# A two-layer spectral and mixer kernel: the d transform split in two steps, four w1 tiles in row halves, and new instruction orders

## The chip, the cores and the metric

The kernel runs on one core of one Trainium2 chip. The metric is the device time of one execution in microseconds. The kernel before the change was run three times: 343.45, 343.85 and 344.21 us, so its median is 343.85 us.

## What is computed

```python
def reference(A_x, A_w_r, A_w_i, B_x, B_w1, B_w2, B_w3, B_w4):
    def _A_ref(x, w_r, w_i):
        B, S, D = x.shape
        X = jnp.fft.rfft2(x.astype(jnp.float32), axes=(-2, -1))
        X = X * (w_r + 1j * w_i)
        return jnp.fft.irfft2(X, s=(S, D), axes=(-2, -1)).astype(jnp.bfloat16)
    def _B_ref(x, w1, w2, w3, w4):
        B, S, D = x.shape
        h = _gelu(_layernorm(x, axis=-1) @ w1)
        c = D // 4
        ...
        hs = jnp.concatenate([g0, g1, g2, g3], axis=-1) @ w2
        x1 = x + hs
        h2 = _gelu(_layernorm(x1, axis=-1) @ w3) @ w4
        return x1 + h2
    x = A_x
    x = x + _A_ref(_layernorm(x, axis=-1), A_w_r, A_w_i)
    x = x + _B_ref(_layernorm(x, axis=-1), B_w1, B_w2, B_w3, B_w4)
    x = x + _A_ref(_layernorm(x, axis=-1), A_w_r, A_w_i)
    x = x + _B_ref(_layernorm(x, axis=-1), B_w1, B_w2, B_w3, B_w4)
    return x
```

S is 2048, D is 512, the hidden width of w3 is 1792, and all inputs are bf16. The quarters g0 to g3 of h are shifted along the sequence by one row down, one up, two down and two up.

## The kernel before

The 2048 rows lie in SBUF as 16 groups "q" of 128 partitions each; row q of the text below means such a group. A layer is the spectral part (a two-dimensional Fourier transform, a product with W, the inverse transform) and the MLP part, and there are two layers; I call them layer 0 (ORDER_A) and layer 1 (ORDER_B).

**The order is written by hand.** Everything of a layer is one string of short operations, and a loop at the end of `layer` (L873) issues them one by one. A letter names the step, a number its tile, a last letter its engine (A for ACT, V for DVE, P for POOL, D for a form on DVE that reads PSUM), and a number after the dot the PSUM bank. Each engine runs its own operations in the order of the string; between engines, semaphores enforce the data dependences. ORDER_0 does the same for the first forward transform (`first_front`, L488). So the order decides what stands ahead of what in each engine's queue.

**The front.** For each row: statistics (`s` on DVE with bn_stats, or, for rows 1, 5 and 9, two sums on ACT), their aggregation (`i` on DVE), for the ACT rows the means and variances on POOL (`f`), the standard deviation per group of rows (`S` on ACT) and its reciprocal (`J` on DVE), then the transform table scaled by it (`Q`, on A, V or P), eight matmuls per row (`O`, L415 to L441), and the copy of the result from PSUM to the tile V (`G` and `L`; V has four parts t, and for split tiles `G` takes parts 0 and 1, `L` parts 2 and 3). One tile of the front is "plain": its right half is copied by ACT (`G3A`), the rest folded by DVE (`G3V`, L454, which writes V's parts 0 and 3 and a tile `pairs`), and a last fold `I` (L464) makes V's parts 1 and 2 out of `pairs`. The three ACT rows' `f2` also issues the first table DMAs on POOL. After ORDER_0 come `load_rest` and `load_mlp` (L553, L554).

**load_rest** (L194) stands in POOL's queue right after the front's last POOL step: a DMA that doubles the first quarter of W, `turn_TL` (L247, which makes the second half of TL for b under 8 out of the first), a second doubling, the DMA of TL2 (the second half of TL for b from 8), then two doublings and two loads of TR. `load_mlp` (L208) on SP waits for the last doubling and then loads G, Tinv and w1 to w3.

**The spectral part.** `d` (L582, four matmuls per b over V's four parts), `t` (its copy to TV), `q` (L602, matmuls of 64 rows that use TL's two halves), `x` (copy to X), `p` (the product with W, on V, P or D), `b` and `V` (L634, over TR), `m` and `l` (copies to hT), `D` and `C` (L656, over G), `Y` (copies), `P` (L679, over Tinv), `a` (L693, adds to x on DVE with a row sum). Units `u` of `d` and `q` hold one or two b's (UNITS, L892).

**The MLP part.** `s` squares on ACT, `r` statistics on POOL, `e` a square root on ACT, `i` the reciprocal, `M` and `n` normalize (A, V or P), `T` transposes two rows by DMA on SP into the tile xT, `v` (L727, w1: 8 matmuls of 512 columns over four rows, i.e. two transposes), `h` (gelu on ACT), `u` (L743, w2, reads neighbouring rows of h), `f`, `k`, `E`, `R`, `o`, `U` the same for the second normalization, `w` (L778, w3), `g` (gelu), `W` (L799, w4), `A` (adds to x). In layer 0 the next layer's front (`B`, `j`, `S`, `J`, `Q`, `O`, `G`, `L`, `I`) is interleaved with w3 and w4. ORDER_B begins with `X6`, six matmuls on zeros (`fill`, L272), and ends with the stores `y`.

Of the kernel before, what the change touches and what calls it, by code (L numbers as in the profile page):

```python
# [567 lines left out]
def layer(K, last):  # L568
# [13 lines left out]
    def over_d(u):  # L582
        bs = UNITS[u]
        ps["d", u] = o = banks(K, len(bs))
        for i, b in enumerate(bs):
            oi = o[:, i].rearrange("p (e r f) -> p e r f", e=2, r=4)
            part = lambda k: V[:, k, 2 * b:2 * b + 2].rearrange("d b q c -> d (b q c)")
            nc.tensor.matmul(oi[:, :, 3], lhsT=part(1), rhs=K.FL[:, 0:P].rearrange("p (e f) -> p e f", e=2),
                             start=True, stop=True)
# [82 lines left out]

    def fold_D(m):
        Y[m] = K.stream.tile([P, 2, 512], BF16, name="Y", tag="TV_Y", bufs=4, padded_shape=[P, 2, 512])
        o, r = ps.pop(("D", m))[:, :, 0:256], Y["r", m][:]
        for h, op in ((0, ALU.add), (1, ALU.subtract)):
            nc.vector.tensor_tensor(Y[m][:, :, h * 256:(h + 1) * 256], o, r, op=op)

    def back_p(q):  # L679
        ps["P", q] = o = banks(K, 1)[:, 0]  # L680
        y = Y[q // 2][:, q % 2]
        if q // 2 in FOLD[last]:
# [44 lines left out]
    def w1(k):  # L727
        g, h = divmod(k, 2)
        ps["v", k] = o = banks(K, 2)
        for i in range(2):  # L730
            j = 2 * h + i
            for t in range(4):
                nc.tensor.matmul(o[:, i], lhsT=K.w1[:, t, j * P:(j + 1) * P], rhs=xT[g][:, :, t, :],  # L733
                                 start=(t == 0), stop=(t == 3))
# [126 lines left out]
    def act_table(k):  # L861
# [5 lines left out]
    table = {"z": act_table, "e": lambda g: ln[g].std_twice(), "i": lambda g: ln[g].invert_twice(), "M": lambda g: ln[g].shift(), "J": invert4, "d": over_d, "t": take_d, "q": over_q, "x": take_q, "p": weigh, "b": lambda b: back_q(b, first_half(b)), "V": lambda b: back_q(b, 1),  # L867
# [4 lines left out]
             "O": front, "G": take_front, "L": lambda k, eng: take_front(k, eng, 1), "I": fold_front, "K": half_D, "H": fold_D, "N": negate}  # L872
# [31 lines left out]
FLEX = "mlGLnotxYIKEpQ"  # L904
FOLD = [(), ()]
ORDER_0 = """
s1 f0 s0 s3 s2 i3 i2 i0 s4 s5 S1 J1 s7 S0 J0 s6 i7 f2 Q2A Q3A i4 Q0A s9 i6 s8 O1.2 s11 f3 S2 J2 Q6P Q1A Q5A O0.4 i8
G1A Q4V O2.0 s10 i11 i10 S3 Q7P O3.2 G0A s13 J3 Q10V Q11A s12 s14 i12 O5.6 i14 G3A i13 G2A Q8P Q9P s15 S4 J4 O4.4 G5A
i15 Q12V Q13V S5 O6.0 L5A J5 Q14P O7.6 G4A G6A G3V Q15V L6V G7A O8.0 L7A G8A I3V L8A
"""  # L910
ORDER_A = """
d0.3 t0A d2.4 d1.2 d4.0 q0.6 t1V N0 t2A q1.2 d6.4 t4A q2.0 x1V x0V p1V t6A q4.2 d12.6 d10.4 x2A p2P p0V t12A t10A d8.0
p4D b0.6 d14.7 q10.4 m0V q6.2 t8A x10A t14A b1.0 b5.1 m5A m1A q12.4 q14.6 p6D b4.1 b2.0 p10V x14A p14P d15.2 m4A m2A
t15A q8.6 x8A b3.1 b7.0 m7A b11.2 q15.6 m11A x15A b10.3 b14.0 m3A b6.2 m6A p12D V12.4 b12.5 p8V p15V b13.7 b9.1 m10A
m12A b8.6 b15.2 m13V V15.3 m14V m9A m8V V13.5 V14.0 m15A D1.6 l12V D0.1 l15A l13A l14V C1 C0 Y0V Y1A D3.3 C3 P3.0 a3
P2.6 Y3A a2 s3 P0.5 a0 s2 P1.2 a1 s0 D2.0 C2 Y2V s1 r0 D5.6 C5 P7.2 a7 Y5A e0 s7 P6.4 D7.0 P4.5 a6 i0 M0 P5.2 D4.6 C4
P10.3 s6 C7 n2P a4 s4 a5 n3V n0V s5 Y4A D6.4 r1 P11.2 C6 P8.6 P9.7 e1 n1V a10 T1 Y7A P15.0 i1 M1 n5A s10 n4P n6P P14.1
Y6V P13.3 a8 s8 T0 a9 n7P s9 a11 P12.4 a15 s11 v1.6 r2 n10P T2 h1 T3 a13 a12 n11V c0 s15 T5 n8V v0.2 h0 s13 v3.4 n9V
v2.2 h3 u0.0 s12 h2 u1.4 a14 c1 s14 T4 u3.1 r3 f0 k0 n14V v5.2 n13A n15V T7 f1 E1V h5 f3 v4.6 u2.0 f2 E2V h4 c2 u6.6
f6 u5.5 f5 E5V k3 E6V n12P u7.0 E0V u4.1 f4 T6 v7.5 k2 k1 R0 E3V o2V o1V h7 o3A c3 v6.1 h6 o0P f7 u8.0 f8 E8P u13.5  # L920
u12.2 u11.6 u14.3 U1 f12 k4 k5 k7 f14 E14V k12 k6 u9.2 f11 u10.4 k8 E7V f13 k13 f10 R1 o7P o5P u15.3 E10V U0 w4.0 E4P
f9 E9P k11 f15 w2.4 g2 k10 o4V U2 w1.2 k14 g4 E15P k9 E13P w3.6 g3 g1 w5.0 w0.4 g0 w6.6 g5 g6 E11V W1.2 o6P U3 E12V A1
W3.6 A3 B3 B1 w8.0 W2.4 A2 W0.2 k15 R2 o10P o11A R3 o14V o9A g8 o12A w13.0 U5 w7.6 B2 g13 o8P U4 w15.4 w10.0 A0 B0 g10
w16.2 j1 g7 g16 w18.0 g18 w9.2 o15P w11.0 g9 w12.2 g12 j3 w17.6 j2 j0 S0 Q3V Q1V Q2P Q0V g11 W4.2 U7 O1.0 o13P g17 U6
A4 W7.3 B4 j4 G1A G1V A7 B7 j7 O0.0 w19.6 G0A W6.2 A6 g19 W5.3 A5 g15 B5 w23.4 g23 j5 B6 j6 S1 Q4P G0V w27.2 g27 I0V
w14.6 g14 Q5V O2.0 w20.2 w24.6 g20 W10.2 A10 B10 Q7V j10 W8.3 G2A A8 B8 W9.4 A9 B9 Q6V j9 W11.2 A11 w26.4 I1P B11 j11
g24 j8 O3.2 w22.6 S2 Q10P g26 G2V I2P Q11A Q8P g22 w21.0 g21 G3A w25.6 G3V g25 W12.0 A12 B12 j12 Q9P S12 J12 I3P O4.5
G4A Q12A G4V W15.1 A15 I4P B15 j15 W13.2 A13 S15 J15 B13 j13 W14.3 Q15P W24.2 S13 J13 Q13P O5.0 A14 A24 B14 B24 j14
G5A O15.4 G15V O6.2 S14 J14 L15A Q14A O14.4 G6A L6A G14A G5V I5V L14A
"""  # L930
# [47 lines left out]
```

## Time and profile before

| | |
|---|---|
| median of three runs | 343.85 us |
| the profiled execution's own time | 343.63 us |
| its span | 341.8 us |
| granted TensorE clock | 1.0 of full speed in every stage |
| TensorE idle before the first front matmul | 8.23 us from the start, 30 fill matmuls aside |
| first `d` matmul, layer 0 | 18.96 us |
| first `D` matmul, layer 0 | 36.87 us |
| first w1 matmul, layer 0 | 51.16 us |
| first `d` matmul, layer 1 | 182.08 us |
| last matmuls end | 339.1 us |

The busy time of an engine is the time in which one of its instructions ran; a matmul's row gives some 270 ns for 256 columns because it is pipelined, though the next one starts after 109 ns. So a busy TensorE is read by the distance from start to start. A waits view tells which engine sat idle for whom; a timeline shows one engine's instructions, start and duration in us, and in brackets the idle time ahead of it and what ended it.

### The profile page before, as it was taken

To read this page: it belongs to the slowest core of one execution; us is meant where nothing else is said; L and a number is where in the kernel's file an instruction comes from. 1 tells how busy PE (TensorE), PEld (TensorE's weight loads), DVE (VectorE), ACT (ScalarE), POOL (GpSimd) and SP (SyncE) were. 2 spreads that over 40 slices of the span, in tenths; PEclk is the share of its full clock that TensorE was granted. 3 is DMA by queue.
4 is the path that set the end of the run, shared out by engine and by line. 5 is a ranking of instruction groups with operands and counts; after the bars stand their busy time and mean duration, and the time that the engine had idled before them with its cause. 6 is when DMAs were issued, how large, how long until landed. Compare 5 with 4: busy or idle time off the path is not lost.

```text
span 341.8 us, 5734 instructions
## 1 busy us (share of the span) xinstructions
PE 334.3 (98%) x2184; PEld 186.8 (55%) x2184; DVE 163.5 (48%) x373; ACT 192.0 (56%) x356; POOL 117.5 (34%) x218
## 2 busy tenths in 40 slices
PE   6999999999999999999999999999999999999996
PEld 4878984444444444444467898444444444444443
DVE  4979895659034023535378979456901110200112
ACT  6989899665821542421628979986695132142310
POOL 3795067669633000402432505877722000000000
PEclk9999999999999999999999999999999999999999
DMA  7985936390231100000000003543130500000011
GB/s 261 313 284 197 339 78 117 71 270 19 46 61 31 32 0 0 2 0 0 2 0 2 2 3 64 104 83 61 33 61 0 125 31 0 15 17 32 15 63 46
DMA packets 45340, 24.60 MB, mean 72 GB/s; under 512 B 35153, under 2 KB 42321, under 8 KB 45313
## 3 DMA queue, kind: packets, MB, share of 16 engines
q1 hardware_dynamic: 43824, 19.74, 23.0%
q0 software_dynamic: 1248, 4.40, 3.9%
q8 instruction: 17, 0.28, 0.3%
q10 hardware_dynamic: 240, 0.10, 0.1%
q14 instruction: 11, 0.08, 0.1%
HBM read 11.61 MB, written 2.10 MB: 40 GB/s over the span
## 4 chain that ended last, share of the span: by engine, by line
PE 85%; ACT 8%; DVE 3%; DMA 2%; issue 1%; SPq 0%; ACTq 0%
PE ps L804 28%; PE ps L784 28%; PE ps L749 8%; PE ps L733 6%; PE ps L642 4%; ACT xn L303 3%; PE ps L612 2%; PE ps L594 2%; DVE x_state L698 2%; PE ps L662 2%; DMA x_state<-in_A_x_dram 1%; ACT hT L740 1%; DMA xT<-xn 1%; PE ps L439 1%; PE ps L429 1%
## 5 line engine op out<-in xcount | busy, mean ns | idle before, releaser
L791 ACT ACTIVATE gT<-ps 128x1024 bf16<-128x1024 f32 x56 | 55.7, 1023 | 97.6 <-PE ps L784 95.5
L804 PE MATMUL ps<-w,gT 128*128 128x512 bf16 (+2 forms) x476 | 99.4, 366 | 0.0
L784 PE MATMUL ps<-xT,w 128*128 128x512 bf16 x448 | 99.3, 379 | 0.0
L810 DVE TENSOR_TENSOR x_state<-ps,x_state 128x512 bf16<-128x512 f32 (+2 forms) x34 | 22.1, 659 | 123.4 <-PE ps L804 123.1
L804 PEld LDWEIGHTS <-gT 128*128 128x128 bf16 x476 | 45.4, 98 | 51.4
L784 PEld LDWEIGHTS <-w 128*128 128x128 bf16 x448 | 43.7, 98 | 52.1
L757 DVE SCALAR_TENSOR_TENSOR xn<-xn,ln_c,ps 128x512 bf16<-128x512 bf16 x32 | 23.3, 742 | 16.0 <-PE ps L749 6.3
L733 PE MATMUL ps<-xT,w 128*128 128x512 bf16 x128 | 28.6, 379 | 0.4 <-DMA xT<-xn 0.4
L749 PE MATMUL ps<-w,hT 128*128 128x512 bf16 x128 | 28.8, 379 | 0.1
L326 POOL TENSOR_SCALAR ln_ve<-ln_mv 128x4 f32<-128x4 f32 x11 | 3.0, 271 | 57.7 <-DVE ln_mv L319 57.0
L303 ACT ACTIVATE junk<-xn 128x512 bf16<-128x512 bf16 x32 | 19.8, 623 | 5.0 <-DVE xn L757 5.0
L291 DVE BATCH_NORM_STATS2 ln_st<-x_state 128x6 f32<-128x512 bf16 (+2 forms) x30 | 19.5, 665 | 3.5 <-DMA x_state<-in_A_x_dram 3.0
L698 DVE SCALAR_TENSOR_TENSOR x_state<-ps,x_state 128x512 bf16<-128x512 f32 x32 | 20.6, 684 | 0.9 <-PE ps L690 0.9
L733 PEld LDWEIGHTS <-w 128*128 128x128 bf16 x128 | 12.4, 98 | 15.6 <-DMA xT<-xn 1.0
L749 PEld LDWEIGHTS <-hT 128*128 128x128 bf16 x128 | 12.5, 98 | 15.4 <-ACT hT L740 1.0
L303 ACT ACTIVATE xn<-x_state 128x512 bf16<-128x512 bf16 x32 | 19.9, 626 | 0.8 <-DVE x_state L698 0.8
L740 ACT ACTIVATE hT<-ps 128x512 bf16<-128x512 f32 x32 | 17.6, 600 | 4.6 <-PE ps L733 4.5
L690 PE MATMUL ps<-Y,Tinv 128*128 128x256 bf16 x128 | 15.8, 272 | 0.4 <-DVE Y L152 0.4
L631 POOL TENSOR_TENSOR PB<-X,W 128x2048 bf16<-128x2048 bf16 (+1 forms) x4 | 12.1, 3033 | 11.2 <-DVE X L152 7.3
L154 ACT ACTIVATE TV<-ps 128x1024 bf16<-128x1024 f32 (+1 forms) x17 | 14.6, 895 | 2.4 <-PE ps L594 2.3
L642 PE MATMUL ps<-TR,PB 128*128 128x128 bf16 x256 | 15.9, 219 | 0.0
L662 PE MATMUL ps<-G,hT 128*128 128x256 bf16 x128 | 15.6, 273 | 0.0
(96 smaller groups left out, 414.0 us busy)
## 6 DMA issues: line engine op xcount, KB each, us to landing
w<-in_B_w_dram SPq DMA_DIRECT2D x4, 896.0 KB, 7.0
W<-W POOLq DMA_DIRECT2D x4, 514.0 KB, 5.1
x_state<-in_A_x_dram SPq DMA_DIRECT2D x8, 256.0 KB, 4.9
out_dram<-x_state SPq DMA_DIRECT2D x15, 128.0 KB, 1.8
w<-in_B_w_dram SPq DMA_DIRECT2D x4, 256.0 KB, 4.4
W<-in_A_w_r_dram SPq DMA_DIRECT2D x7, 128.5 KB, 5.4
W<-in_A_w_i_dram SPq DMA_DIRECT2D x7, 128.5 KB, 5.6
TL<-tab_TL POOLq DMA_DIRECT2D x3, 256.0 KB, 5.5
```

Source lines behind the costliest of these rows:

```text
L303: K.nc.scalar.activation(out, src, ACT.Square, bias=0.0, scale=D ** -0.5, accum_out=self.s[:, i, 1:2])
L642: nc.tensor.matmul(o[:, k0 * P:(k0 + 1) * P], lhsT=pab[u][:, k, 2 * (b - u) + h, f * P:(f + 1) * P], rhs=K.TR[:, k:k + 2, 2 * b + h], star ...
L662: nc.tensor.matmul(o[:, i, e * 256:(e + 1) * 256], lhsT=M[:, F, e, 2 * m + i, :], rhs=K.G[:, F, e, :], start=(F == 0 and e == 0), stop=(F ...
L698: nc.vector.scalar_tensor_tensor(K.x[:, q, :], ps.pop(("P", q)), 1.0, K.x[:, q, :], op0=ALU.mult, op1=ALU.add, accum_out=ln[g].s[:, i, 0:1])
L733: nc.tensor.matmul(o[:, i], lhsT=K.w1[:, t, j * P:(j + 1) * P], rhs=xT[g][:, :, t, :], start=(t == 0), stop=(t == 3))
L740: nc.scalar.activation(hv[:, 2 * h + i, 4 * g:4 * g + 4, PAD:PAD + P], o[:, i].rearrange("p (q c) -> p q c", q=4), ACT.Gelu_apprx_tanh, bi ...
L749: nc.tensor.matmul(o, lhsT=K.hT[:, j, st:st + P], rhs=K.w2[:, j, :], start=(j == 0), stop=(j == 3))
L757: nc.vector.scalar_tensor_tensor(xn[:, q, :], xn[:, q, :], ln[q // 4].c[:, q % 4:q % 4 + 1], ps.pop(("u", n)), op0=ALU.mult, op1=ALU.add, ...
L784: nc.tensor.matmul(o[:, i], lhsT=K.w3[:, c, t * P:(t + 1) * P], rhs=xT3[g][:, :, c, :], start=(c == 0), stop=(c == 3))
L791: nc.scalar.activation(gT[g][:, 2 * j:2 * j + 2, :], ps.pop(("w", k)), ACT.Gelu_apprx_tanh, bias=0.0, scale=1.0)
L804: nc.tensor.matmul(o, lhsT=gT[g][:, t, i * P:(i + 1) * P], rhs=K.w4[:, t, d], start=(t == 0), stop=(t == 13))
L810: nc.vector.tensor_tensor(x, ps.pop(("W", n)), x, op=ALU.add)
```

## The change

`over_d` becomes two operations: `d` multiplies V's parts 1 and 0, `F` parts 3 and 2 of the same bank. `w1` for k = 0 and 1 in each layer multiplies rows 0 and 1 (`v0`, `v1`) and rows 2 and 3 (`v8`, `v9`) separately. The tables get a way to fold the inverse transform on POOL (`whole_D`, `fold_P`, POOL_FOLD), which is empty and called by no order. All three orders are new; among others, the six fill matmuls of ORDER_B are gone, `I3` is on POOL in ORDER_0 and `Q14` there on ACT. Shown are the code and the parts of the orders that are spoken of.

```diff
--- before.py
+++ after.py
@@ -579,19 +579,23 @@
     ps = {}
     tv, X, pab, Y, xT, xT3, gT, ln, ln3, lnA = [{} for _ in range(10)]
 
-    def over_d(u):
+    def over_d(u, late):
         bs = UNITS[u]
-        ps["d", u] = o = banks(K, len(bs))
+        if not late:
+            ps["d", u] = banks(K, len(bs))
+        o = ps["d", u]
         for i, b in enumerate(bs):
             oi = o[:, i].rearrange("p (e r f) -> p e r f", e=2, r=4)
             part = lambda k: V[:, k, 2 * b:2 * b + 2].rearrange("d b q c -> d (b q c)")
-            nc.tensor.matmul(oi[:, :, 3], lhsT=part(1), rhs=K.FL[:, 0:P].rearrange("p (e f) -> p e f", e=2),
-                             start=True, stop=True)
-            nc.tensor.matmul(oi[:, :, 1], lhsT=part(2), rhs=K.FL[:, P:2 * P].rearrange("p (e f) -> p e f", e=2),
-                             start=True, stop=True)
-            for k in range(2):
-                rhs = K.FL[:, (k + 1) * 256:(k + 2) * 256].rearrange("p (e r f) -> p e r f", e=2, r=2)
-                nc.tensor.matmul(oi[:, :, 0:3:2], lhsT=part(3 * k), rhs=rhs, start=(k == 0), stop=(k == 1))
+            k = 2 if late else 1
+            single = lambda: nc.tensor.matmul(oi[:, :, 1 if late else 3], lhsT=part(k), start=True, stop=True,
+                                              rhs=K.FL[:, (k - 1) * P:k * P].rearrange("p (e f) -> p e f", e=2))
+            if not late:
+                single()
+            rhs = K.FL[:, (late + 1) * 256:(late + 2) * 256].rearrange("p (e r f) -> p e r f", e=2, r=2)
+            nc.tensor.matmul(oi[:, :, 0:3:2], lhsT=part(3 * late), rhs=rhs, start=not late, stop=bool(late))
+            if late:
+                single()
...
 
+    def whole_D(m, eng):
+        Y["r", m] = K.grp.tile([P, 2, 512], FP32, name="whole", tag="xT", bufs=4)
+        copy(K, Y["r", m][:], ps.pop(("D", m)), eng)
+
+    def fold_P(m):
+        Y[m] = K.stream.tile([P, 2, 512], BF16, name="Y", tag="TV_Y", bufs=4, padded_shape=[P, 2, 512])
+        r = Y["r", m]
+        for h, op in ((0, ALU.add), (1, ALU.subtract)):
+            nc.gpsimd.tensor_tensor(Y[m][:, :, h * 256:(h + 1) * 256], r[:, :, 0:256], r[:, :, 256:512], op=op)
+
     def fold_D(m):
+        if m in POOL_FOLD[last]:
+            fold_P(m)
+            return
         Y[m] = K.stream.tile([P, 2, 512], BF16, name="Y", tag="TV_Y", bufs=4, padded_shape=[P, 2, 512])
         o, r = ps.pop(("D", m))[:, :, 0:256], Y["r", m][:]
@@ -679,7 +696,7 @@
     def back_p(q):
         ps["P", q] = o = banks(K, 1)[:, 0]
         y = Y[q // 2][:, q % 2]
-        if q // 2 in FOLD[last]:
+        if q // 2 in FOLD[last] + POOL_FOLD[last]:
...
@@ -725,12 +742,18 @@
             K.load_w4()
 
     def w1(k):
+        rows = slice(0, 4)
+        if k % 8 in V_HALVES:
+            rows = slice(0, 2) if k < 8 else slice(2, 4)
+        k, late = k % 8, k >= 8
         g, h = divmod(k, 2)
-        ps["v", k] = o = banks(K, 2)
+        if not late:
+            ps["v", k] = banks(K, 2)
+        o = ps["v", k].rearrange("p i (q c) -> p i q c", q=4)
         for i in range(2):
             j = 2 * h + i
             for t in range(4):
-                nc.tensor.matmul(o[:, i], lhsT=K.w1[:, t, j * P:(j + 1) * P], rhs=xT[g][:, :, t, :],
+                nc.tensor.matmul(o[:, i, rows], lhsT=K.w1[:, t, j * P:(j + 1) * P], rhs=xT[g][:, rows, t, :],
                                  start=(t == 0), stop=(t == 3))
...
 PLAIN = 6
-FLEX = "mlGLnotxYIKEpQ"
+FLEX = "mlGLnotxYIKEpQZ"
 FOLD = [(), ()]
+POOL_FOLD = [(), ()]
+V_HALVES = (0, 1)
 ORDER_0 = """
-s1 f0 s0 s3 s2 i3 i2 i0 s4 s5 S1 J1 s7 S0 J0 s6 i7 f2 Q2A Q3A i4 Q0A s9 i6 s8 O1.2 s11 f3 S2 J2 Q6P Q1A Q5A O0.4 i8
-G1A Q4V O2.0 s10 i11 i10 S3 Q7P O3.2 G0A s13 J3 Q10V Q11A s12 s14 i12 O5.6 i14 G3A i13 G2A Q8P Q9P s15 S4 J4 O4.4 G5A
-i15 Q12V Q13V S5 O6.0 L5A J5 Q14P O7.6 G4A G6A G3V Q15V L6V G7A O8.0 L7A G8A I3V L8A
+s0 i0 s1 f0 s5 f2 s2 s3 s4 S0 i3 i2 s7 S1 s9 J0 Q1A J1 Q3A Q2A Q0V s6 i4 O0.3 i7 i6 s11 s10 S2 J2 G0A f3 s8 i11 Q4V
+O1.6 i8 i10 Q5A s13 S3 J3 Q11P s12 Q7A i13 Q6A s14 i14 i12 Q10A O2.0 s15 Q9V G1A G2A O3.4 S4 G3A O5.2 Q8P i15 S5 J4
+O4.6 Q13V Q12V J5 Q15A Q14A G3V I3P O6.0 G5V G4A L6A O8.4 G8A L8A O7.6 L7A G6V G7V L5V
 """
 ORDER_A = """
-d0.3 t0A d2.4 d1.2 d4.0 q0.6 t1V N0 t2A q1.2 d6.4 t4A q2.0 x1V x0V p1V t6A q4.2 d12.6 d10.4 x2A p2P p0V t12A t10A d8.0
-p4D b0.6 d14.7 q10.4 m0V q6.2 t8A x10A t14A b1.0 b5.1 m5A m1A q12.4 q14.6 p6D b4.1 b2.0 p10V x14A p14P d15.2 m4A m2A
-t15A q8.6 x8A b3.1 b7.0 m7A b11.2 q15.6 m11A x15A b10.3 b14.0 m3A b6.2 m6A p12D V12.4 b12.5 p8V p15V b13.7 b9.1 m10A
-m12A b8.6 b15.2 m13V V15.3 m14V m9A m8V V13.5 V14.0 m15A D1.6 l12V D0.1 l15A l13A l14V C1 C0 Y0V Y1A D3.3 C3 P3.0 a3
...
-g24 j8 O3.2 w22.6 S2 Q10P g26 G2V I2P Q11A Q8P g22 w21.0 g21 G3A w25.6 G3V g25 W12.0 A12 B12 j12 Q9P S12 J12 I3P O4.5
-G4A Q12A G4V W15.1 A15 I4P B15 j15 W13.2 A13 S15 J15 B13 j13 W14.3 Q15P W24.2 S13 J13 Q13P O5.0 A14 A24 B14 B24 j14
-G5A O15.4 G15V O6.2 S14 J14 L15A Q14A O14.4 G6A L6A G14A G5V I5V L14A
+d0.0 d2.4 d1.7 F1 t1A F0 F2 d4.2 F4 N0 t2A t0V q0.6 x0A q1.0 d6.4 F6 t4V q4.6 q2.2 x1A t6A p0V d12.0 x2A d10.4 F10 F12
+d8.2 p1V F8 p4D p2P t10A q10.4 q6.6 t12A b4.0 x10A d14.1 m4A t8V p6D d15.2 F14 t14A F15 t15A b0.4 b1.5 q14.0 q8.2 m0A
+q12.6 m1A x14A q15.4 x8A p10V b6.0 x15A b11.1 m11A b5.2 b3.3 m5A m6A p14P b10.4 b14.5 b7.2 b2.0 m10A p12D m7A b13.1
+m3A b12.4 p8V m13A b8.2 b9.7 p15V m2V b15.3 m12A m14V V15.6 V12.1 m15V l15V m8A V14.5 l14V V13.0 m9A D1.3 l13A D0.6
+l12V C1 C0 Y0V D3.0 C3 Y1A P2.2 a2 P3.3 a3 P0.6 P1.4 a0 a1 Y3A P6.5 P7.1 s2 D2.2 a7 C2 s3 s0 s1 r0 Y2V s7 e0 D4.0 C4
+Y4A D7.6 P4.4 i0 a6 M0 n0P a4 P5.2 n1P a5 P8.3 a8 n2V s6 s4 s5 D5.0 C5 C7 s8 r1 e1 D6.2 C6 P9.4 Y5V P11.5 i1 n3V Y6A
...
+Q7A Q4V O2.4 w27.6 O3.0 g24 G2A G3A G3V G2V g27 I3P W15.2 A15 W12.1 B15 j15 A12 B12 I2P S15 J15 j12 Q15V S12 J12 W13.4
+A13 B13 j13 S13 Q12V J13 Q13P W14.1 A14 W24.0 A24 B14 B24 j14 O15.5 G15V S14 O6.0 J14 L15A Q14V L6V G6A O14.2 L14V
+G14A
 """
 ORDER_B = """
-X6.7 d4.4 d15.7 t15A d12.2 t4V d1.0 d0.1 q15.4 t1V q4.6 t12A x15V q1.2 t0A x4A d2.0 p15P p1D q0.4 p0D q12.6 d10.2 t2A
...
-m12A m8V m14V V12.0 V14.1 V15.3 V13.2 m10A m6A l14V m11A l12A D2.5 l15V l13A D3.0 C3 Y3A C2 D1.2 C1 Y2V Y1A P7.1 a7
-P6.0 a6 P4.5 P5.7 P2.2 P3.3 D0.0 s7 a4 s6 C0 a5 D5.4 s4 s5 r1 C5 a3 s3 Y0V D6.6 a2 e1 P0.0 P1.2 i1 a0 a1 Y5A P10.1 M1
...
-g18 W7.6 A7 y7 W4.4 A5 A4 y4 y5 w19.6 g19 y15 W9.1 A9 W8.3 y9 W11.0 A11 y11 W10.5 W20.4 A8 y8 A10 y10 A20 y20
+d15.5 d4.6 F4 F15 t15V t4A d12.2 d1.0 F12 d0.1 F1 t1V F0 q15.4 x15V q4.6 t12A t0A q1.2 p1D p15P x4A d2.0 F2 q0.4 x0V
...
+b10.6 m3A m0A p14V m8A m11A m13V m7V b14.7 m6A b12.3 V14.1 V13.5 m10V m12V V15.4 V12.0 m14A D3.2 l15A l14V D2.6 l13V
+l12A C3 Y3A C2 Y2V D1.0 C1 P6.5 P4.3 P5.2 a6 Y1A a4 a5 s6 P7.5 D0.0 C0 s4 D4.6 C4 a7 Y0V s5 P2.2 P3.3 P1.5 P0.4 s7 Y4A
+D5.0 r1 C5 a2 D6.6 e1 i1 M1 a3 a0 C6 D7.3 C7 s2 s3 n4P P9.2 n5V T2 Y5A s0 P10.0 a1 s1 n6P P11.1 n7V T3 Y6V P12.6 r0 a9
+Y7A e0 i0 M0 n1P s9 a10 P13.7 n0A s10 a11 P15.2 s11 P8.3 a8 s8 P14.5 a14 r2 n11P v2.0 h2 T0 n3V v3.4 h3 n2V a15 T1 a13
+s14 c0 s13 v1.2 v0.0 v9.6 h1 a12 v8.2 n10V h0 u3.5 u1.4 T5 n9V n8V T4 f1 c1 u2.0 s15 f2 E2V s12 v5.1 r3 v4.6 h5 u4.2
...
+W10.6 W20.2 A8 y14 y8 A10 y10 A20 y20
 """
```

## The prediction

> **What bounds the kernel now.** I read the page first: busy times, then the chain that ended last.
>
> ```profile
> PE 334.3 (98%) x2184; PEld 186.8 (55%) x2184; DVE 163.5 (48%) x373; ACT 192.0 (56%) x356; POOL 117.5 (34%) x218
> ...
> PE 85%; ACT 8%; DVE 3%; DMA 2%; issue 1%; SPq 0%; ACTq 0%
> ```
>
> TensorE is busy for 98% of the span and carries 85% of the chain, so the time is TensorE's work plus its holes. I take what a matmul costs from the distance between two starts in the timeline: 216 ns for 512 columns, 109 for 256, 56 for 128. Summed, TensorE starts a matmul about as fast as it can from 19 us to the end. The granted clock is 1.0 in every stage. Next I read who TensorE waited for:
>
> ```profile
> engine line waited for: us in total, times, longest us
> PE ps L429 <- ACT Tq L412: 2.4, 2, 1.9
> PE ps L274 <- DVE zeros L265: 1.0, 1, 1.0
> PE ps L733 <- DMA xT<-xn: 0.4, 2, 0.3
> PE ps L690 <- DVE Y L152: 0.4, 1, 0.4
> PE ps L588 <- DVE V L471: 0.3, 1, 0.3
> ```
>
> Only the last three lie behind the front, 1.1 us. This view leaves out holes under 150 ns and those that pipelining covers. Counted from start to start, less 109 ns or 216 ns for the matmul itself, the holes behind the front are: 0.28 us at 18.96 (the first `d` waits for V), 0.32 at 50.7 and 0.27 at 58.9 (layer 0, first w1 and w2 tiles), 0.14 at 128.5, then 0.15 at 180.5, 0.65 for the six fill matmuls and 0.17 at 182.1 (layer boundary), 0.60 and 0.17 at 207 and 0.46 at 214.0 (layer 1, inverse transform and first w1 tile). That is 3.2 us. One more price shows here: on the way into a run of `q` matmuls (64 rows) a start-to-start distance is 205 ns in place of 109, on the way out 202 in place of 109, 0.19 us a run.
>
> Last I read POOL's queue from the end of the front on, because the change moves steps on it:
>
> ```profile
> start us, us, engine line op out<-in xcount [idle before <-releaser]
> 16.22 0.93 POOL L410 TENSOR_SCALAR Tq<-T,ln_r 128x256 bf16<-128x256 bf16 x1 [1.70 <-PE ps L429]
> 17.09 0.67 POOL L185 DMA_DIRECT2D W<-W  x1
> 17.77 0.18 POOL L197 COPY gate<-Tq 1x2 bf16<-1x2 bf16 x1
> 17.93 1.63 POOL L250 TENSOR_SCALAR TL<-TL 128x512 bf16<-128x512 bf16 x1
> 19.49 0.75 POOL L251 COPY TL<-TL 128x512 bf16<-128x512 bf16 x1
> 20.16 0.67 POOL L185 DMA_DIRECT2D W<-W  x1
> 20.83 0.57 POOL L200 DMA_DIRECT2D TL<-tab_TL  x1
> ```
>
> The reader is to see a serial chain: the front's last POOL step (`Q14P`), then `load_rest`. Its `turn_TL` (L250, L251) makes the second half of TL that `q0` multiplies with; it ends at 20.24, `q0` starts at 21.3. The TL2 transfer issued at 20.83 lands at 26.15, `q10`, the first unit with b over 7, starts at 26.6. W's last doubling lands at 31.21, `p14P` starts at 31.34. The tables arrive just ahead of use, with 1.1, 0.5 and 0.1 us to spare.
>
> **The change, part by part.** *Two-part d.* Same four matmuls for each b, so 0 on TensorE; `d` needs only V's first half and `F` the second. It can remove the 0.28 at 18.96 and shorten the layer boundary. *Half tiles of w1.* Four tiles (k = 0, 1, both layers) of 8 matmuls become 16 each: 16 x 109 - 8 x 216 = 16 ns a tile, 0.06 us in all; the 32 more weight loads lie beside 109 ns streams, as those of L690 (256 columns, starts 109 ns apart) already do. `whole_D`, `fold_P` and POOL_FOLD are called by no order: 0. *Fewer q runs.* 6 to 4 in layer 0, 5 to 5 in layer 1: -0.38 us.
>
> *The new front.* I lay out the new order by hand with the trace's durations. ACT is the bound: row 9's sums (two of 0.61) now come before the first Tq, from the landing at 7.86 to 9.12. Then come Q1, Q3, Q2 (0.40 each), S2 (0.19), G0 (0.90), Q5, a wait until 12.0 for row 10's statistics, S3, Q7 and Q6 (0.31 each), Q10, G1, G2, S4, G3's right half (0.48): S5 at 15.7, J5 on DVE at 16.05 (before: 15.86). TensorE starts at 8.4 (Q0 on DVE), waits 0.6 us for Q1 as before, and has done the fronts at 18.9; `d0` waits for G7's half on DVE until 19.18. Before, `d` effectively started at 18.96 + 0.28 = 19.24. So the front is worth -0.06; the bounds are -0.5 and +0.5, as one missed statistics step on ACT or DVE costs 0.6.
>
> *What moved on POOL.* `Q14P` leaves POOL and `I3P` comes: it needs `pairs` of `G3V`, which stands behind J5. G3V took 1.33 us before (15.94 to 17.27), so now 16.13 to 17.46; I3P then takes 2 x 0.73, overlapping by 0.05, until 18.9. `load_rest` starts at 18.9 instead of 17.09, and with it all its DMAs: +1.8. With the chain's own lengths (turn ended 3.15 after its start, TL2 landed 9.06 after), turn ends at 22.05 and TL2 lands at 27.95.
> TensorE reaches `q0` at 19.18 + 6 blocks x 0.33 = 21.16, and waits 0.9. It reaches `q10` without this wait at 25.9 (t10 on ACT), and so waits until 27.95. Behind it are queued in order all other matmuls; after `q10` begins there are 10 b of q (0.218 each), 2 b of d (0.33), 16 b of b (0.448), 10.0 us, plus 0.28 for run edges and 0.25 of small changes of kind (before as well). `b14` waits some 0.3 more: W's last doubling, 33.0 instead of 31.2, then p14P's 1.92. The first `D` starts at 38.8 in place of 36.87: **+1.9**, front and saved runs included. Without the table waits it would be 36.87 - 0.06 - 0.38 = 36.4.
>
> The Trainium skill speaks for a smaller sum. Its page DMA: Bandwidth & Descriptors (section on the anatomy of a SWDGE DMA) fits a GpSimd DMA by about 2.0 us and its bytes over 436 GB/s. For TL2's 256 KB that is 2.6 us; issued by 23.2, it would land at 25.8, ahead of `q10`, and only the 0.9 at `q0` were left. The row of this kernel:
>
> ```profile
> DMA to landing us min/median/max: 5.3/5.5/5.9
> ```
>
> This is TL's, and TL2's own was 5.3. The doubling of W ahead of TL2 in the same queue is moving until 22.9, and the DMA engines are 93 to 100% busy from 23 to 29 us. The order in the queue stays, so I take 5.3. The bounds of the +1.9 are +0.5 by the page and +2.3 if POOL is held up beside DVE once more (a step of L471 on DVE took 0.79 instead of 0.43 beside L250).
>
> *Layer 0, inverse transform to w2.* With half tiles w1 starts on T0's rows alone. By hand from the first D: row 0 to 3's sums, r0, e0, i0, then n0P and n1P on POOL put T0 at +9.6, and the transposes land 3.2 us after issue (46.68 to 49.93): +12.8 against TensorE at +12.65; the second w2 tile waits 0.25 for ACT (h2). 0.45 remains of 0.59: -0.15. The hole at 128.5: -0.1.
>
> *Layer boundary.* The six fills go (-0.65), but O5 (0.45) is now done earlier and no longer covers the last row's statistics: from W24's end, Q14 on DVE comes at +2.3 where O15 and O6 cover 1.98, and the first `d` waits 0.3 for G14. `d` starts 3.3 us after W24 against 4.06, less the 0.45 of O5 moved out: -0.3. If the idle array lost its clock the fills would have been worth keeping; the 1.90 us idle at 6.3 left the clock at 1.0 and these holes are shorter, so 0.
>
> *Layer 1.* Its tables are long in place. The folds into P4 and P1 are fed in time but for 0.17, T2 is issued at +9.6 by the same steps as T0, T3 1.3 later, and both have landed as v2 is reached (+14.1), about 0.25 more around u1 and v2: 0.4 remains of 1.23, -0.8. The stages of w3 and w4 have no holes to win; bounds 0 and +0.4, since w6 is reached as U1 lands.
>
> Sum: +1.9 - 0.15 - 0.1 - 0.3 - 0.8 + 0.06 = +0.6. On the profiled execution (343.63 with a span of 341.8) 344.2; it lies 0.2 under the median of 343.85, so **344.4** against the median.
>
> **Rivals.** *The tables are in time* (faster). If I3P runs early, or DMAs speed up with the W loads from SP over by 21.4, the waits at q0 and q10 vanish: -0.44 - 1.35 + 0.06 = -1.7, 342.1; with the page's landing 0.9 of it stays, 343.0. For it: DMA is busy only 0.7 at 19 to 23 us. Against: G3V cannot precede J5. *The same lag, and the gains lost* (slower): the w1 start in layer 1 misses its transposes because the normalizing steps queue behind Y casts on DVE and ACT, which gives back the 0.8 and opens 0.4 more: +0.6 + 1.2 = +1.8, 345.6. It decides once T2 is issued over 0.8 us later than the +9.6 after layer 1's first D that I reckon. *The half tiles do nothing*: if k = 0 still waits for both transposes, +1.3 on the main case, 345.7; but reads and writes are of separate rows.
>
> **How the numbers follow.** The likeliest, 0.45, is the lag with the gains: 344.4, by itself 343.6 to 345.2. Tables in time or partly so 0.34, around 342.1; the two slower rivals 0.21, around 345.6. The range of 8 in 10 is 341.8 to 345.8. A measurement tells about 0.2%, 0.7 us, from no change: faster 0.36 (the first rival and a little of the main case), within 0.2 (what of the main case stays below 344.5), slower 0.44.
>
> **What would show it.** After: POOL's first DMA of load_rest at about 18.9, L251 ending near 22, TensorE holes before the first L612 and before `q10` of together 2 us, first L662 at 38.8; no L274 at the boundary; holes before the first w1 tile of layer 1 under 0.3. I am wrong if POOL's load_rest starts by 17.5, or TL2 lands by 26.

## The result and the profile after

The changed kernel takes 346.35 us (median of 6, 345.99 to 346.94) against 343.81 (6 runs, 343.11 to 344.21): ratio 1.0078, 95% interval 1.0064 to 1.0092, so 2.5 us slower. The forecast of 344.4 had the direction and a quarter of the size, and its range ended 0.55 us too low. The profiled execution took 346.0 us with a span of 344.2, at a clock of 1.0. In some executions of the runs below the granted clock was 0.994 or 0.995 instead of 1.0 (in run 7's profile 0.91 to 0.92 up to 20 us and 1.0 behind) and the time 0.3 to 2.2 us above the median of the same kernel's others, so figures "at clock 1.0" leave these executions out.

The page's rows for busy time and for the chain that ended last:

```profile
PE 333.8 (97%) x2210; PEld 189.6 (55%) x2210; DVE 165.4 (48%) x378; ACT 192.9 (56%) x356; POOL 118.5 (34%) x215
...
PE 85%; DMA 8%; ACT 3%; SPq 1%; DVE 1%; issue 1%; POOL 0%; ACTq 0%; POOLq 0%
```

TensorE does the same work (26 matmuls more: 32 from the halves, 6 fills fewer), but DMA now has 8% of the chain instead of 2%. POOL's timeline from the end of the front on:

```profile
17.50 1.41 POOL L471 TENSOR_TENSOR V<-pairs 128x256 bf16<-128x256 f32 x2 [2.92 <-DMA W<-in_A_w_r_dram]
18.87 0.67 POOL L185 DMA_DIRECT2D W<-W  x1
...
19.71 1.84 POOL L250 TENSOR_SCALAR TL<-TL 128x512 bf16<-128x512 bf16 x1
21.48 0.74 POOL L251 COPY TL<-TL 128x512 bf16<-128x512 bf16 x1
...
22.83 0.57 POOL L200 DMA_DIRECT2D TL<-tab_TL  x1
```

I3P (L471) stands ahead of load_rest, which starts at 18.87 instead of 17.09; the whole queue of tables behind it is 1.8 to 2.0 us later than before (TL2 was issued at 20.83, now at 22.83). And TensorE's waits:

```profile
engine line waited for: us in total, times, longest us
...
PE ps L616 <- DMA TL<-tab_TL: 1.0, 1, 1.0
...
PE ps L756 <- DMA xT<-xn: 0.7, 1, 0.7
PE ps L807 <- DMA xT<-xn: 0.5, 1, 0.5
PE ps L616 <- POOL TL L251: 0.4, 1, 0.4
```

The two L616 rows are `q10` and `q0`, waiting for the tables. The L756 row is layer 1's first w1 tile on T3, and the L807 row is a place that had no wait before: w3's tile 6 in layer 1 (`w6`), the first product on the transpose U1.

By the starts of the stages' first matmuls, before and after, the 2.4 us of the span fall to:

| stretch | forecast | profiles |
|---|---|---|
| up to the first D of layer 0 (36.85, now 38.82) | +1.9 | +1.97 |
| layer 0, D to w3 (u15, 0.86 us, moved behind w3's start, counted alike) | -0.15 | -0.07 |
| layer 0, w3 to layer 1's first d (u15 counted alike) | -0.4 | -0.32 |
| layer 1, d to D (17.28, now 17.54) | 0 | +0.26 |
| layer 1, D to w1 (15.21, now 15.11) | -0.8 with the row below | -0.10 |
| layer 1, w1 to w3's tile 6 (27.64, now 28.31) | | +0.67 |
| behind it | 0 | 0 |
| sum (half tiles +0.06 in the forecast) | +0.6 | +2.41 |

Nearly all of the miss, 1.6 of 1.8 us, lies in layer 1, where +0.83 stands in place of -0.8. The experiments ask what the tables cost, and what happened in layer 1.

### The profile page after: what moved, and what is told of

It reads as the page before. It is cut to its first block, busy times and chain, and to the rows that moved or that the text cites. A ratio compares the mean times of both kernels' runs of the same rounds, so it can differ in the third digit from the quotient of the medians.

```text
span 344.2 us, 5770 instructions
## 1 busy us (share of the span) xinstructions
PE 333.8 (97%) x2210; PEld 189.6 (55%) x2210; DVE 165.4 (48%) x378; ACT 192.9 (56%) x356; POOL 118.5 (34%) x215
## 4 chain that ended last, share of the span: by engine, by line
PE 85%; DMA 8%; ACT 3%; SPq 1%; DVE 1%; issue 1%; POOL 0%; ACTq 0%; POOLq 0%
PE ps L807 28%; PE ps L827 28%; PE ps L756 8%; PE ps L772 7%; PE ps L646 4%; DMA W<-in_A_w_i_dram 3%; PE ps L666 3%; PE ps L707 2%; DMA xT<-xn 2%; DMA TL<-tab_TL 2%; PE ps L616 1%; ACT xn L303 1%; DMA W<-in_A_w_r_dram 1%; PE ps L596 1%; PE ps L439 1%; SPq L243 1%
## 5 line engine op out<-in xcount | busy, mean ns | idle before, releaser
L807 PE MATMUL ps<-xT,w 128*128 128x512 bf16 x448 | 99.5, 379 | 0.5 <-DMA xT<-xn 0.5
L807 PEld LDWEIGHTS <-w 128*128 128x128 bf16 x448 | 43.8, 98 | 53.0 <-issue 0.7
L756 PE MATMUL ps<-xT,w 128*128 128x512 bf16 (+1 forms) x160 | 29.0, 337 | 0.7 <-DMA xT<-xn 0.7
L756 PEld LDWEIGHTS <-w 128*128 128x128 bf16 x160 | 15.4, 98 | 13.1 <-DMA xT<-xn 1.5
L635 POOL TENSOR_TENSOR PB<-X,W 128x1024 bf16<-128x1024 bf16 (+1 forms) x5 | 14.4, 2891 | 9.9 <-DVE X L152 6.7
L787 POOL TENSOR_TENSOR x_state<-x_state,xn 128x512 bf16<-128x512 bf16 x14 | 16.4, 1178 | 3.4 <-DVE xn L780 3.4
L429 PE MATMUL ps<-Tq,x_state 128*128 128x256 bf16 (+1 forms) x144 | 12.8, 246 | 3.2 <-DMA x_state<-in_A_x_dram 2.7
```

What stands on the lines that cost most here:

```text
L756: nc.tensor.matmul(o[:, i, rows], lhsT=K.w1[:, t, j * P:(j + 1) * P], rhs=xT[g][:, rows, t, :], start=(t == 0), stop=(t == 3))
L807: nc.tensor.matmul(o[:, i], lhsT=K.w3[:, c, t * P:(t + 1) * P], rhs=xT3[g][:, :, c, :], start=(c == 0), stop=(c == 3))
```

## The experiments

**1. The start order of before, in the changed kernel.**

```
-ORDER_0 = """ s0 i0 s1 f0 s5 ... I3P O6.0 ... """
+ORDER_0 = """ s1 f0 s0 s3 s2 ... I3V L8A """
```

> The changed kernel with the first forward transform in the order of before (I3 on DVE, Q14 on POOL), all else as changed. Table theory (I3 on POOL sends load_rest, and with it every table DMA, 1.8 us later): load_rest starts at 17.1 us again, TL2 lands near 26.2, the first D of layer 0 starts at 36.4 to 36.9 instead of 38.8, and the time falls by 1.9 us, to 344.4. Rival (the split d and its order make layer 0's start slow): the first D stays at 38.3 or later and the time within 0.5 us of 346.35.

Measured: 344.54 us (11 runs), ratio to before 1.0029 (1.0017 to 1.0042), 1.8 us less than the changed kernel. The time is as expected. load_rest starts at 17.16 and TL2 lands at 26.19. The first D was expected at 36.4 to 36.9 and came only at 37.79 in the profiled execution, which at 345.22 us was one of the four longest of the eleven. There the waits for TL are gone, but `q6` waited for p4D on DVE, whose product needs W's second doubling (landed at 24.29, product begun at 24.77):

```profile
PE ps L616 <- DVE PB L632: 0.4, 1, 0.4
```

**2. The start order of after, in the kernel before** (the same lines the other way round).

> The kernel before with the first forward transform in the order of the change, all else as before. Table theory: load_rest at 18.9, TL2 at 28.1, the first D of layer 0 about 1.9 us later than 36.85, the time 345.5 to 345.9. Rival (the loss comes from the order behind the front): the time within 0.5 us of 343.8.

Measured: 345.70 us (6 runs, 344.13 to 346.63), ratio 1.0056 (1.0034 to 1.0078), 2.0 us more than before. At clock 1.0 (344.13, 344.44 and 345.23) it is only 0.8 us more by the median, and so is the span of the profile, 342.6 against 341.8. load_rest starts at 18.74 and TL2 lands at 27.66, near what was expected; the first D comes at 37.74, only 0.9 us later, where 1.9 were expected. The waits behind the front, in part:

```profile
PE ps L588 <- DVE V L152: 0.9, 1, 0.9
...
PE ps L612 <- DMA TL<-tab_TL: 0.2, 1, 0.2
```

The undivided `d` of the kernel before needs all of V: its first one waits for the last copy to V, which ends at 19.80, and starts at 19.85 instead of 18.96; from there to the first D it takes 17.89 us in both kernels. So here the late front hides nearly all of the tables' lag. The start order is worth 1.8 us by taking it out of the changed kernel and 0.8 by putting it into the one before.

**3. TL2's transfer ahead of load_rest's other steps.**

```
 def load_rest(after):
+    q.dma_start(K.TL[:, 1, 8:16], dram["TL2"])
     double(0)
 ...
     double(1)
-    q.dma_start(K.TL[:, 1, 8:16], dram["TL2"])
```

> The changed kernel with TL2's DMA as the first of load_rest instead of the third; W's doublings follow. If the wait of q10 for TL2 is itself what costs (1.2 us in the trace), the first D of layer 0 comes 1.2 us earlier and the time falls to 345.1. If the whole chain of tables sets the end (W's last doubling lands at 33.1 as before, p14 on POOL and b14 wait for it), q10's hole only moves to b14, the first D stays within 0.3 us of 38.8 and the time within 0.4 us of 346.35.

Measured: 346.11 us (5 runs), ratio 1.0071 (1.0059 to 1.0084): within 0.3 us of the changed kernel. TensorE's waits behind the front:

```profile
PE ps L616 <- POOL TL L251: 0.9, 1, 0.9
...
PE ps L616 <- DVE PB L632: 0.3, 1, 0.3
```

The wait for TL2 is gone; the one for the turned half is longer by 0.5, as the transfer's own issue of 0.60 us stands ahead of the turn, and then the products wait for W's doublings. The first D comes at 38.43 instead of 38.82, but 0.34 of that is a front that was earlier in this execution (first `d` at 19.12 instead of 19.46). One late table was not the cost: POOL's whole queue is late, and each of its steps has a reader close behind it.

**4. Layer 1's halves on the tiles that come first.** In layer 1's order tiles 2 and 3 come before 0 and 1, so V_HALVES = (0, 1) splits tiles that do not come first.

```
-V_HALVES = (0, 1)
+V_HALVES = ((0, 1), (0, 1, 2, 3))
-        if k % 8 in V_HALVES:
+        if k % 8 in V_HALVES[last]:
 ORDER_B:
-v2.0 h2 T0 n3V v3.4 h3 n2V
+v2.0 v3.4 v10 h2 T0 n3V v11 h3 n2V
```

> The changed kernel with the first two w1 tiles of layer 1 (k = 2 and 3, which its order takes first) multiplied in row halves as well, the late halves behind the early ones. If the hole of 0.86 us ahead of layer 1's first w1 tile is the wait for the second transpose (T3 lands at 216.26, T2 at 214.43), it goes, part of it comes back at later tiles that wait for T1 (lands 220.99), and the time falls by 0.3 to 0.8 us. If both transposes or the gelu behind them set the pace anyway, the time stays within 0.2 us of 346.35.

Measured: 345.13 us (5 runs), ratio 1.0045 (1.0033 to 1.0057), 1.2 us less: more than expected. The 0.86 us hole ahead of w1 is gone (0.33 comes back at a later tile). So is the hole of 0.62 ahead of w3's tile 6, which this edit has nothing to do with by its data. The next runs are about that.

**5. Edits 1 and 4 together.**

> Both edits that won something put together: the start order of before (alone 344.54 us against 346.35 of the changed kernel, so 1.8 us) and layer 1's halves on the tiles that come first there (alone 345.13, so 1.2 us). They lie in stages 170 us apart. If the change's loss is the lag of the tables plus two holes of layer 1, the two gains add: 346.35 - 1.8 - 1.2 = 343.3 us, level with before or 0.4 us under it. Rival: the two gains overlap, because layer 1's holes close when the core comes to them at another time (the run with the start order of before had holes of 1.0 and 1.1 us there): then it stays at 344.3 to 344.6 us.

Measured: 343.40 us (21 runs), ratio to before 0.9992 (0.9985 to 0.9999). The gains add, so the rival is out. The first D comes at 37.20. Over the profiles at clock 1.0 that have the changed layer 0, it comes at 37.95 to 39.14 with the new start order (7 profiles, median 38.82) and at 36.85 to 37.79 with that of before (runs 1, 5, 10 and 12, median 37.05): 1.8 us again, of which 0.5 lies ahead of the first `d`.

**6. The residual add of row 3 moved from POOL to DVE (E3P to E3V), with the normalisations of rows 3 and 2 earlier.**

```
 ORDER_B:
-f6 o0V c3 u13.4 f13 u15.7 f5 E3P o3V o2V E13V
+f6 o0V E3V o3V o2V c3 u13.4 f13 u15.7 f5 E13V
```

> Layer 1 alone: the residual of row 3 goes from POOL to DVE and stands, with the normalisations of rows 3 and 2, ahead of the next two residual adds. In the changed kernel's profile those two normalisations end at 240.75 us, since the POOL operation ran until 239.74 and two DVE additions stood ahead; the transpose of their pair was issued at 240.77 and landed at 244.58, and the first w3 product on it started at 244.62 after a hole of 0.84 us. Theory: the chain over that POOL operation makes the hole, and with it 1 us earlier the hole of 0.6 us beyond a matmul's own time goes: 345.7 to 345.9 us. Rival: the pair ahead of it, which waits for ScalarE's gelu and its squares, lands at 243.55 at the earliest and DVE's added 0.3 us delays what follows, so nothing is won: 346.2 to 346.5 us.

Measured: 346.19 us (5 runs), ratio 1.0073 (1.0061 to 1.0086): as the rival said. Rows 3 and 2 were normalised by 237.22, 3.5 us earlier, and the hole ahead of tile 6 grew from 0.62 to 0.99 us. The SP queue's timeline and the transposed tile's landings in that stretch say why:

```profile
238.29 2.74 SPq L735 DMA_TRANSPOSE xT<-xn  x2
```

```profile
DMA to landing us min/median/max: 4.4/4.7/5.0
```

U1 stands behind U0 in SP's queue, and U0 waits for ScalarE. Then the two take 5.0 and 4.4 us to land, where most transposes of this kernel take 3.0 to 3.3. The theory of the hole fails here; the cause has to be sought in the transfer.

**7. No halves in layer 0.**

```
-V_HALVES = (0, 1)
+V_HALVES = ((), (0, 1))
 ORDER_A:
-v1.2 a11 s11 a10 v0.6 T1 ... P15.4 v9.2 h1 n4V T3 a15 T2 s15 v8.6 ... P13.2 h0
+a11 s11 a10 T1 ... P15.4 P13.5 v1.2 h1 n4V T3 a15 T2 s15 v0.6 ... h0
```

> The changed kernel with w1's first two tiles of layer 0 undivided (tile 1 starts where its second half stood, product 13 of the inverse transform goes ahead of it); nothing else is moved. Theory: in layer 0 the halves are on the tiles that really come first and let 8 matmuls of 256 columns (0.9 us) run before the second pair of rows has landed, so without them 0.5 to 0.9 us comes back as a hole: 346.9 to 347.3 us. Rival: halves do nothing in layer 0 either, the product ahead of them fills the same time: 346.2 to 346.5 us.

Measured: 346.09 us (6 runs), ratio 1.0073 (1.0060 to 1.0086), by the time nearest to the rival. By its profile both are half right: layer 0 from D to w3 takes 42.18 us instead of 41.30, the upper end of the 0.5 to 0.9 expected, and layer 1 from w1 to w3 27.67 instead of 28.31, although nothing in layer 1 was edited. The hole ahead of tile 6 has gone.

**8. Layer 1's order of before, in the changed kernel** (each `d` followed by its `F`, w1 undivided there).

```
-V_HALVES = (0, 1)
+V_HALVES = ((0, 1), ())
-ORDER_B = """ d15.5 d4.6 F4 F15 ... """
+ORDER_B = """ X6.7 d4.4 F4 d15.7 F15 ... """
```

> The changed kernel with layer 1's order as it was before (its d transform's two operations follow each other directly, and w1's tiles are undivided there); start and layer 0 are the changed ones. By the two profiles layer 1 from its first d to its last matmul takes 157.6 us after and 157.0 before. Theory: layer 1's new order is 0.6 us to the bad, where 0.8 us of gain had been forecast: 345.6 to 345.9 us. Rival: the new order is no worse, and the old one has its own holes (1.23 us in the profile of before, 0.7 of it at 207 us) that come back: 346.3 to 347 us.

Measured: 346.38 us (6 runs), ratio 1.0084 (1.0069 to 1.0100): the rival's time, but the loss is in a place where neither theory had it. Layer 1's d part is back to 17.12 us; then a new hole of 1.5 us stands at 219, behind a transpose that took 4.8 us.

**What the late transposes share.** Runs 4 and 7 took away a hole in a stretch that they didn't touch; in run 6 that hole grew, and run 8 had a long one in another place. The trace of the DMA queues of the changed kernel, 238 to 246 us in 40 slices of 0.2 us (first row busy tenths of the 16 DMA engines, second row GB/s):

```profile
DMA  0000000000008999998089990002991000000000
GB/s 0 0 0 0 0 0 0 0 0 0 0 1 172 219 214 216 195 206 171 17 173 214 187 55 8 9 10 58 280 287 15 0 0 0 0 0 0 0 0 0
...
q1 hardware_dynamic: 2112, 0.52, 46.0%
q8 instruction: 1, 0.02, 0.8%
issues: line engine op xcount, KB each, median us to landing
xT<-xn SPq DMA_TRANSPOSE x2, 4.1
```

One packet of 16 KB on queue 8, a load of instructions, runs from 241.75 to 242.77. In the middle of the transposes the rate falls from some 215 to 8 to 10 GB/s for 0.6 us. A sixteenth of 215 is 13, so fifteen of the engines seem to have finished, and the transfer to wait for the one that carries the load. These loads come every 23 to 28 us in the matmul stages, about as long as TensorE takes for 256 instructions (a weight load and a matmul for each 216 ns step make 27.6 us). Over the profiles of the two kernels and the twelve experiments, transposes issued after 45 us took 3.14 us (median of 377) with no load of instructions (16 KB on queue 8 or 8 KB on queue 14) between 1.3 us after their issue and their landing, and 5 of these over 3.4; with one the median of 71 is 3.74, the longest 5.0, and 52 took over 3.4. The hole ahead of w3's tile 6 follows this in every profile: in the five with a 16 KB load in the flight of U0 and U1 (the changed kernel and runs 1, 3, 6 and 10) it is 0.62 to 0.99 us, and in the nine others it is not there. In run 4 the load came at 237.81, ahead of the transposes, and in run 7 at 246.83, behind their landing. The Trainium skill's page Runtime: NRT & Kernel Launch, section on instruction fetch mechanics, says that the program comes in blocks of 16 KB (256 instructions) over a DMA queue of the sequencer's own, and calls the cost mostly hidden. The block agrees with the packet of 16,384 bytes. For TensorE the cost is hidden here: no hole stands behind 245 us, where three more loads come. For a transfer in flight it is not.

If so, the length of TensorE's program ahead of a transpose decides whether it is hit, and an edit of the wake-up matmuls, whose result nothing reads, must move the holes.

**9. Fewer wake-up matmuls, as long in time, in the changed kernel.**

```
-    fill(K, WAKE)
+    for i in range(WAKE):
+        nc.tensor.matmul(K.ps[:, 7, 0:512], lhsT=t[:], rhs=t[:].unsqueeze(1).to_broadcast([P, 4, P]), start=True, stop=True)
-WAKE = 30
+WAKE = 15
```

> The changed kernel with 15 wake-up matmuls of 512 columns at the start instead of 30 of 256: TensorE is busy just as long, but its program is 30 instructions shorter, and nothing else is touched. In the changed kernel's trace one load of instructions (16 KB, queue 8, 241.75 to 242.77 us) falls into the two transposes issued at 239.22 and 240.77, which land after 4.3 and 3.8 us instead of 3.1. Theory: these loads come each 256 TensorE instructions, so this one moves some 3 us later, past the transposes' landing; they take 3.1 us again, the hole ahead of w6 (0.84 us) goes, and the time falls by about 0.6 us, to 345.6 to 345.9 us. Rival: the transposes are late for another reason (the order of layer 1) and the length of the program is nothing: 346.2 to 346.5 us with the hole in place.

Measured: 345.11 us (6 runs, 344.53 to 346.68), ratio 1.0056 (1.0034 to 1.0078); 345.0 at clock 1.0 (4 runs), where the changed kernel has 346.3 (5 runs). The view of the DMA queues from 237 to 245 us:

```profile
DMA  0000000000000000799999509999994000000030
GB/s 0 0 0 0 0 0 0 0 0 0 0 0 0 0 0 0 155 219 209 220 201 200 107 13 180 219 212 216 204 197 71 0 0 0 0 0 0 0 82 0
...
q8 instruction: 1, 0.02, 0.8%
issues: line engine op xcount, KB each, median us to landing
xT<-xn SPq DMA_TRANSPOSE x2, 3.1
```

The load now comes at 244.8, after both transposes (the 82 GB/s near the end of the row); they take 3.1 us, and TensorE no longer waits for them. The stretch from w1 to tile 6 is 27.68 instead of 28.31. The median fell by 1.2 us, more than the 0.6 us of this stretch, and its interval overlaps that of the changed kernel, so the size rests on the profile.

**10. The same edit in kernel 5** (the kernel of run 5).

> The same edit of the wake-up matmuls in the kernel with the start order of before and the halves on the first tiles (343.4 us). There the load in question lies at 236.1 us, ahead of the transposes issued at 237.1 and 238.7, which land after 3.1 us. Theory: 30 instructions fewer move that load by some 3 us to about 239.4, into their flight: they take 4 us or more, a hole of 0.5 to 0.9 us opens ahead of w6, and a hole of 0.4 at 219 us, whose transpose was hit by the load at 216.3, may close: 343.6 to 344.2 us, so the same edit that helps the changed kernel hurts this one. Rival: no effect, 343.3 to 343.5 us.

Measured: 344.07 us (22 runs), ratio 1.0007 (0.9998 to 1.0015) against 0.9992 (0.9985 to 0.9999): 0.15% or 0.5 us slower, with intervals that just touch. From 236 to 244 us:

```profile
DMA  0000000002999999159997000009940000000000
GB/s 0 0 0 0 0 0 0 0 0 42 216 219 215 197 205 177 27 106 311 204 106 8 1 8 9 10 10 269 292 72 0 0 0 0 0 0 0 0 0 0
...
xT<-xn SPq DMA_TRANSPOSE x2, 4.5
```

The load moved from 236.1 to 239.7, into the transposes' flight, and a hole of 0.93 us opened ahead of tile 6, which kernel 5 did not have:

```profile
PE ps L808 <- DMA xT<-xn: 0.8, 1, 0.8
```

The one edit takes the hole out of one kernel and puts it into the other, each time as the load moves. This part of the cause is shown.

**11. Kernel 8 with 18 wake-up matmuls of 384 columns** (as run 9, with WAKE = 18 and `[P, 3, P]`).

> The changed kernel with layer 1's old order (346.38 us) and 18 wake-up matmuls of 384 columns instead of 30 of 256. In the run without the second edit a load at 218.08 to 219.16 us lay in the flight of the transpose issued at 215.93, which landed after 4.8 us, with a hole of 1.7 us at 219. Theory: 24 instructions fewer move the load to about 220.7, past that landing and ahead of the next transposes' packets; that hole shrinks by over 1 us, layer 1 takes as long as in the kernel before (142.4 us from its first D to its last matmul end of 341.8), and the time is 345.2 to 345.5 us, so that the old order of layer 1 is 0.3 to 0.4 us better than the new one with the same freedom from loads. Rival: the hole is the old order's own behind the changed layer 0: 346.2 to 346.5 us.

Measured: 346.15 us (6 runs), ratio 1.0078 (1.0065 to 1.0091); the time expected was missed. In the profile the load moved to 220.7, the transposes hit before took 3.9 and 3.5 us (another queue's load of 8 KB remains in their flight), the hole at 219 shrank from 1.5 to 0.2 us and w1 to w3 by 1.2; but the median fell by only 0.2 (at clock 1.0 from 346.13, 4 runs, to 345.64, a single one). Whether layer 1's old order is the better one with equal freedom from loads stays open: by the profiles from layer 0's first D to the start of the last matmul it is 0.4 us better than run 9 (301.47 against 301.84), and by the time at clock 1.0, that of a single run, 0.6 us worse.

**12. Kernel 5 with layer 1's d part in the order of before** (up to `D2.6 l15V l13A D3.2`, then as kernel 5).

```
 ORDER_B:
-d15.5 d4.6 F4 F15 ... l14V D2.6 l13V l12A
+d4.4 F4 d15.7 F15 ... l12A D2.6 l15V l13A D3.2
```

> Start order of before, layer 0 of the changed kernel, and in layer 1 the d transform and the products up to its first D in the order of before (its two operations following each other directly), with the changed order behind that and the halves on the tiles that come first (343.40 us with the new order of the d part). By the profiles layer 1's d part takes 17.1 us in the old order and 17.5 in the new, in the changed kernel and in the one with layer 1's old order. TensorE's program has the same length as in the 343.40 us kernel, so its loads of instructions stay where they were, ahead of the transposes at 237 us. Theory: 0.4 us less, 342.9 to 343.1 us, 0.2% under the kernel before. Rival: what the d part gives up comes back as a wait for the transposes at 215 us, whose loads are at fixed places of the other engines' programs: 343.3 to 343.6 us.

Measured: 343.56 us (14 runs), ratio 0.9994 (0.9985 to 1.0002): the rival's figure. The wait that came back is another than it named: TensorE waits 0.5 us at 198 for a cast of hT on DVE, ahead of the first D, and the d part takes 17.9 us. Kernel 5 and this one, both 0.2 us under the kernel before in their median, cannot be told apart.

## Why the prediction was right about the front and wrong about layer 1

*What bounds the kernel.* Right: TensorE's work and its holes. By these the stages add up to the 2.41 us of the span.

*The new front and POOL's queue.* Right in its mechanism, and to 0.2 us: load_rest at 18.87 (forecast 18.9), L251's end at 22.22 (22.05), TL2 landed at 28.08 (27.95), the first D at 38.82 (38.8). That the last agrees to 0.02 is luck in part: with the same start order it comes between 37.95 and 39.14, the first `d` came at 19.46 instead of 19.18, and the two holes at the tables were 0.58 and 1.22 us, 1.8 where the forecast had 2.05. Taking the start order out won 1.8 us (run 1); the 36.4 that the forecast had without table waits was not reached (36.85 at best, run 10). Putting it in cost 0.8 us (run 2), in another layer 0 and for the most part by the wait for V. I3P on POOL is one step of 1.4 us in a queue whose every result has a reader within a microsecond or so, and run 3 shows that no single table carries it; no run moved I3P alone, so its share of the start order's 1.8 us is argued.

*The choice against the page DMA: Bandwidth & Descriptors of the Trainium skill.* TL2 took 5.25 us in the changed kernel, where the sum of its section on the anatomy of a SWDGE DMA gave 2.6, an estimate. In run 3, issued ahead of the others, it took 3.5 us, the least of these rows:

```profile
DMA to landing us min/median/max: 3.5/5.8/6.0
```

So most of the distance between the row and the page goes when TL2 stands first in POOL's queue; some 0.9 us stays, while W's loads from SP, the last landing at 21.1, still share the engines.

*Layer 0 and the boundary.* -0.07 and -0.32 against -0.15 and -0.4: right. The half tiles there do win 0.9 us of stage time (run 7): they are on the tiles that come first.

*"Layer 1. ... 0.4 remains of 1.23, -0.8."* This step failed: of 0.8 us, the stretch from D to w1 gained 0.10. The holes at 207, 0.77 us, shrank to one of 0.23 at 204.5, but one of 0.86 stands at 216, where the forecast had both transposes landed as v2 is reached, at +14.1 from layer 1's first D. TensorE was ready at +14.25; T3 landed at +15.06. T2 was issued at +10.0 (forecast +9.6), T3 1.35 later (1.3), and T3 took 3.7 us to land, where the forecast had taken 3.2 from layer 0. The chain of the kernel before had shown 3.5 at this very place:

```profile
211.02 3.50 DMA xT<-xn
```

and that of the changed kernel has

```profile
212.57 3.69 DMA xT<-xn
```

So about half of the lateness is the issue and half the landing. Two 8 KB loads of queue 14 lie in T3's flight, and 0.6 of the 0.86 would go with a landing after 3.1. In all ten profiles with the changed order from layer 1's first D on they begin 3.2 to 3.3 and 3.8 to 4.2 us behind T2's issue, in runs 9 and 10 too, so they are not moved by the length of TensorE's program, and T3 takes 3.66 to 3.80; no run moved them, so this share is argued. The halves could not help: ORDER_B has v2 and v3 undivided ahead of them, so that its first tile needs both transposes, as the forecast's own "as v2 is reached" has it; with the halves on those (run 4) the hole goes.

*"The stages of w3 and w4 have no holes to win; bounds 0 and +0.4, since w6 is reached as U1 lands."* This failed too: the stretch from w1 to tile 6 grew by 0.67 us. The forecast saw that there was no slack, but its bound of 0.4 left no room for a landing so late. The load of instructions hit both transposes: 4.3 and 3.8 us, a hole of 0.62. Runs 9 and 10 show it.

*The rivals.* "The same lag, and the gains lost" came nearest in its figure, 345.6, and is not what happened: its mark was T2 over 0.8 us later than +9.6, and T2 was 0.4 later. "The tables are in time" is out. "The half tiles do nothing" is wrong for layer 0 (run 7); in layer 1 they stand behind the tiles that wait, a reason that it didn't name.

*What stays open:* the +0.26 in layer 1's d part. Some 0.19 of it is one pause at 200.43, just ahead of the first D, for an ACT copy to hT that ends at 200.38; with the old order (run 8, 17.12 us) it is not there, and in run 12 a longer wait for such a copy stands in its place. Also open are I3P's own share of the start order and the moving of queue 14's loads.

## What to carry to other kernels

A step added to a queue that also issues transfers delays everything behind it, here by 1.8 to 2.0 us, so lay out the readers of each item in the queue before you move work there. A split tile helps only where it is the first that its engine comes to: look it up in the order of each layer. Where a product is reached just as a transfer lands, give that landing a spread from all such transfers in the trace, not its median, and look for instruction loads in its flight before blaming the order around it.

## What the runs showed of the hardware that was not expected

A transpose from SBUF to SBUF lands 3.0 to 3.4 us after its issue (372 of 377), but in 52 of 71 cases 3.5 to 5.0 us after it if a load of instructions comes while it moves; one 16 KB packet of such a load lasts 0.9 to 1.6 us in the stages behind 46 us. Where the load of queue 8 falls depends on the number of TensorE's instructions ahead of it: 30 instructions fewer moved it by 3.0 us (run 9) and 3.5 us (run 10). So an edit of no length in time, as 16 matmuls of 256 columns in place of 8 of 512, can shift a hole of 0.6 to 0.9 us in or out of a stage that lies 25 us (run 4) to 190 us (run 7) further on; half of what run 4 won in its profile (0.62 of 1.17 us) was of that kind.
